# Choosing the place of a first ramp so that four ramps fit one instruction, with a new table for the planner

## The chip, the cores and the metric

One core of a Trainium2 chip. The metric is the time of one execution on the device, in microseconds. The core's engines are called here as the profile calls them: PE (TensorE, matrix products; PEld is its loading of weights), ACT (ScalarE), DVE (VectorE), POOL (GpSimd) and SP (SyncE, which issues the DMAs).

## What is computed

Two layers, each of a multi-query attention (32 heads of 16 columns that share one key and one value head) and a gated MLP with a spatial product over the sequence. The input x is 2048 x 512 in bf16.

```python
def _A_ref(x, wq, wk, wv, wo):
    q = (x @ wq).reshape(B, S, H, Dh)          # H = 32, Dh = 16
    k, v = x @ wk, x @ wv                      # one head
    p = softmax(einsum('bhqd,bkd->bhqk', q, k) * Dh ** -0.5)
    return einsum('bhqk,bkd->bhqd', p, v).reshape(B, S, H * Dh) @ wo

def _B_ref(x, w_in, w_sp, b_sp, w_out):
    z = gelu(x @ w_in)                         # 2 x 896 columns
    g = einsum('ts,bsf->btf', w_sp, layernorm(z[..., 896:])) + b_sp
    return (z[..., :896] * g) @ w_out

for _ in range(2):
    x = x + _A_ref(layernorm(x), ...)
    x = x + _B_ref(layernorm(x), ...)
```

## The kernel before

**Blocks.** The scores of a layer are cut into 2048 blocks of 128 keys by 512 columns (query rows times heads), so 4096 in all. A score matmul (line 2501) makes one block in one of the eight banks of PSUM; up to four stand in a pack and use different rows of PE. A block is then exponentiated into one of 41 places of `Pb` in SBUF (128 x 512 bf16 each, `NPS`), and PV matmuls (line 2758) multiply the places with the values into a bank that gathers four head groups. The values carry a column of ones, so that the denominators come with the products.

**Two ways to exponentiate.** On ACT a block is one Exp from PSUM into a place (line 2698), or two blocks of neighbouring banks go in one instruction (line 2699). [...] A block given to DVE becomes three ramps in int16, whose bits read as bf16 approximate an exponential each; their weighted sum, by weights that three variants of the values hold, is close to the exponential. The first ramp (line 2590, `dve_block` and `first_fn`) reads PSUM and frees the bank. The second and the third (tag "S") read the place of the first and write places of their own; POOL or DVE may take them. A first ramp's place becomes free again when both ramps that read it and its own PV matmul are done.

**Ramps in one instruction.** `commit_ramp` looks for waiting ramps of the same number. Two can always go together (`two`, a step from place to place). Four go together when their sources form a regular box, that is, when of the four places in order the first and the last add up to as much as the two in the middle (`box`), and when four free places form a box too (`free_quad`); the access pattern then has two steps (`quad`). In the profile all of these stand at line 2610 (`ramps_fn`), and their form tells how many: 128x1024 is two, 128x2048 four. A ramp alone is at line 2594. Before the change a first ramp takes the place that has been free longest (`free_slots(1)[0]`).

**The order.** No instruction order is written by hand. While the program is built, a planner (`Sched`, `Kernel.run`) steps through time with a cost for each kind of instruction, and whenever an engine is free in its model, picks what it does next; the order on each engine and the semaphore waits are thereby fixed. For each stretch of 1250 ns of the planner's own time (`STEP`) `follow` sets parameters from `PLAN`: the share of blocks that go to DVE (`SHARE`), how many blocks an Exp may take (`ACT_MAX`), how long a score pack waits to be filled (`FILL_MIN`), whether POOL and DVE may take four ramps at once (`QUADP`, `QUADD`), and some twenty more. A DVE ramp is planned only where POOL is idle in the model, and POOL's next instruction waits for it.

**The stages.** In each layer keys and queries are made first (ramp-up: two groups of blocks run over all keys while keys still arrive). Then packs, exponentials and PV run through all blocks; projections, layer norms, MLP products and spatial products (lines 2181, 2259, 2315, 2354, 2383) are fitted in between on PE. When the last chunk of queries is done, its normalisation, projection, layer norm and MLP follow in a chain, with spatial products beside it (between the layers: the bridge; at the end: the tail). In the second layer's ramp-up no block goes to DVE.

Of the kernel before, what the change touches and what calls it, by code (L numbers as in the profile page):

```python
# [74 lines left out]
def c_mm(n, cols):  # L75
# [8 lines left out]
    11: dict(SLACK=450, PV_MAX=3, PV_LEAST=4),  # L84
    12: dict(SLACK=350, SLACK_HI=400, DVE_LEAD=300),
    13: dict(SLACK=350, SLACK_HI=400, ACT_LOW=1700, FILL_BUSY=4, DVE_LEAD=300, DVE_HIGH=1200),
    14: dict(FILL_MIN=3, MISC_T=2500, QUADD=0),
    15: dict(ACT_LOW=900, PV_LEAST=8),
    16: dict(ACT_LOW=900, PV_LEAST=8, HOLD=400),
    17: dict(ACT_LOW=900, PV_LEAST=8, POOL_TOP=2500, HOLD=400),  # L90
    18: dict(ACT_LOW=900, PV_LEAST=8, SHARE=0.24, POOL_TOP=2500, HOLD=400),
    19: dict(SLACK=450, ACT_LOW=900, PV_LEAST=8, SHARE=0.24, POOL_TOP=2500, HOLD=400),
    20: dict(SLACK=350, SLACK_HI=650, PV_LEAST=4, SHARE=0.24, DVE_LEAD=300, POOL_TOP=2500, MISC_T=700, QUADD=0),
    21: dict(SLACK=350, SLACK_HI=650, PV_LEAST=4, SHARE=0.24, POOL_TOP=2500, MISC_T=700, COLS=2900, DVE_HIGH=1200, QUADD=0),
    22: dict(SLACK=350, SLACK_HI=650, PV_LEAST=4, PV_EFF=0.8, SHARE=0.24, POOL_TOP=2500, MISC_T=700, COLS=2900, DVE_HIGH=1200, QUADD=0),
    23: dict(SLACK=350, SLACK_HI=650, PV_LEAST=4, PV_EFF=0.8, SHARE=0.24, POOL_TOP=2500, MISC_T=700, COLS=2900, DVE_HIGH=1200, QUADD=0),
    24: dict(SLACK_HI=300, ACT_LOW=1700, SHARE=0.31, SCORE_CAP=5, COLS=0, QUADP=0),
    25: dict(SLACK_HI=300, ACT_LOW=1700, SHARE=0.31, SCORE_CAP=5, COLS=0, QUADP=0),
    26: dict(SLACK_HI=300, ACT_LOW=1700, PV_EFF=0.8, SHARE=0.31, SCORE_CAP=5, COLS=0, QUADP=0),
    27: dict(SLACK_HI=300, PV_LEAST=4, COLS=0),  # L100
    28: dict(SLACK=450, FILL_MIN=3, MISC_T=2500),
    29: dict(SLACK=450, FILL_MIN=3, MISC_T=2500, ACT_MAX=1),
    30: dict(PV_LEAST=4),
    31: dict(ACT_MAX=1, QUADD=0),
    32: dict(FILL_MIN=3),
    33: dict(PV_LEAST=4),
    34: dict(PV_LEAST=4, POOL_TOP=3500),
    35: dict(SLACK_HI=400, PV_LEAST=4, POOL_TOP=3500),
    36: dict(SLACK_HI=400, ACT_LOW=1700, PV_LEAST=4, POOL_TOP=3500),
    37: dict(SLACK_HI=400, ACT_LOW=1700, FILL_BUSY=4, PV_LEAST=4, POOL_TOP=3500),  # L110
    38: dict(SLACK_HI=300, PV_MAX=4, PV_LEAST=8, POOL_TOP=2500, ACT_MAX=1, SCORE_CAP=7, DVE_HIGH=2400),
    40: dict(PV_EFF=0.8),
    41: dict(PV_LEAST=4, PV_EFF=0.8),
    42: dict(PV_LEAST=4),
    43: dict(PV_LEAST=4),
    44: dict(PV_LEAST=4, PV_EFF=0.8, MISC_T=700, SCORE_CAP=7),
    45: dict(PV_LEAST=4, PV_EFF=0.8, DVE_LEAD=-600, POOL_TOP=7000, MISC_T=700, SCORE_CAP=7),
    47: dict(PV_MAX=1),
    48: dict(PV_MAX=1),
    49: dict(ACT_LOW=900, COLS=3300, QUADD=0),  # L120
    50: dict(SLACK=600, ACT_LOW=900, FILL_MIN=4, PV_MAX=1, SHARE=0.36, HOLD=400, COLS=0, QUADP=0),
    51: dict(SLACK=600, ACT_LOW=900, FILL_MIN=4, PV_MAX=1, PV_LEAST=4, SHARE=0.36, POOL_TOP=2500, HOLD=400, SCORE_CAP=5, COLS=0, QUADP=0),
    52: dict(SLACK=600, ACT_LOW=900, FILL_MIN=4, PV_MAX=1, PV_LEAST=4, SHARE=0.36, POOL_TOP=2500, HOLD=400, MISC_T=700, SCORE_CAP=5, COLS=0, QUADP=0),
    53: dict(PV_MAX=3, QUADD=0),
    54: dict(FILL_MIN=4, HOLD=400),
    56: dict(SLACK_HI=650),
    58: dict(SLACK_HI=400),
    59: dict(SLACK_HI=400),
    60: dict(SLACK_HI=400),
    61: dict(SLACK_HI=400, PV_MAX=1),  # L130
    62: dict(SLACK_HI=400, PV_MAX=1, MISC_T=2500),
    63: dict(SLACK_HI=400, PV_MAX=1, PV_LEAST=8, PV_EFF=0.8, MISC_T=2500),
    65: dict(PV_LEAST=8),
    66: dict(PV_LEAST=8, POOL_TOP=7000),
    68: dict(FILL_MIN=3, PV_LEAST=4),
    69: dict(PV_EFF=0.8, POOL_TOP=7000),
    70: dict(PV_EFF=0.8, POOL_TOP=7000),
    71: dict(PV_LEAST=8),
    72: dict(PV_LEAST=4, POOL_TOP=2500),
    73: dict(PV_LEAST=4, SHARE=0.24, POOL_TOP=2500),  # L140
    74: dict(FILL_BUSY=3, DVE_LEAD=300),
    75: dict(FILL_BUSY=3, PV_MAX=1, PV_LEAST=8, DVE_LEAD=300),
    76: dict(FILL_MIN=4, FILL_BUSY=3, PV_MAX=1, PV_LEAST=8, DVE_LEAD=300, MISC_T=700),
    77: dict(FILL_MIN=3, FILL_BUSY=3, PV_MAX=1, PV_LEAST=8, SHARE=0.4, DVE_LEAD=300, MISC_T=700),
    78: dict(POOL_TOP=2500),
    80: dict(ACT_LOW=1700, SHARE=0.31, DVE_LEAD=-600),
    81: dict(FILL_MIN=3),
    83: dict(SLACK=450, PV_EFF=0.8, DVE_LEAD=-300),
    85: dict(SLACK=200, SLACK_HI=300, FILL_MIN=3, POOL_TOP=3500),
    86: dict(SLACK=200, SLACK_HI=300, FILL_MIN=3, PV_MAX=3, POOL_TOP=7000),  # L150
    87: dict(SLACK=200, SLACK_HI=300, FILL_MIN=3, PV_MAX=3, POOL_TOP=7000),
    88: dict(PV_MAX=1, DVE_LEAD=-300, DVE_HIGH=2400),
    89: dict(SLACK_HI=800, SHARE=0.24),
    91: dict(HOLD=0, QUADP=0),
    92: dict(DVE_LEAD=-600),
    93: dict(SLACK=450, SHARE=0.24),
    94: dict(ACT_LOW=1700, FILL_MIN=4, PV_MAX=3),
    95: dict(ACT_LOW=500, PV_EFF=0.8, MISC_T=2500),
    96: dict(ACT_LOW=1700, QUADP=0),
    97: dict(HOLD=0, QUADD=0),  # L160
    99: dict(FILL_BUSY=4, DVE_LEAD=300),
    100: dict(FILL_BUSY=4, DVE_LEAD=300, HOLD=0),
    101: dict(FILL_BUSY=4, PV_MAX=1, DVE_LEAD=300, HOLD=0, SCORE_CAP=7),
    103: dict(QUADP=0, QUADD=0),
    104: dict(ACT_LOW=900, PV_MAX=1, QUADD=0),
    105: dict(FILL_BUSY=3, SHARE=0.4, HOLD=400, QUADP=0),
    106: dict(FILL_BUSY=3, PV_LEAST=4, SHARE=0.4, HOLD=400, QUADP=0),
    107: dict(PV_LEAST=4, SHARE=0.4, HOLD=400, QUADP=0),
    108: dict(PV_LEAST=4, SHARE=0.4, HOLD=400, QUADP=0, QUADD=0),
    109: dict(ACT_LOW=1700, PV_LEAST=4, SHARE=0.4, DVE_LEAD=300, HOLD=400, QUADD=0),  # L170
    110: dict(SHARE=0.28),
    112: dict(SLACK=450, SLACK_HI=800, ACT_LOW=1050, PV_LEAST=8, POOL_TOP=2500, HOLD=400, MISC_T=2500, SCORE_CAP=5, DVE_HIGH=1200, QUADD=0),
# [163 lines left out]
    289: dict(FILL_MIN=3),  # L336
    291: dict(DVE_LEAD=-300),
    293: dict(ACT_LOW=1400, FILL_MIN=3, MISC_T=700, DVE_HIGH=2400),
    294: dict(PV_MAX=1, SCORE_CAP=7),
    295: dict(PV_MAX=4),  # L340
    297: dict(QUADD=0),
    298: dict(QUADD=0),
# [2863 lines left out]
```

## Time and profile before

| | |
|---|---|
| runs | 1473.71, 1475.56, 1475.73 us; median 1475.56 us |
| profiled execution | 1473.03 us, its span 1471.3 us |
| instructions | 35574 |
| clock granted to PE | 0.999 of full speed |

The span is the time from the first to the last instruction that the profile has; the execution's own time is 1.7 us longer. A row of instruction groups has the line, the engine, the operation, output and input with their shapes, the count, then busy us and the mean duration in ns, then the engine's idle time before these instructions and what ended it. A row of a stretch has its bounds, its length and the busy time of PE, PEld, DVE, ACT and POOL with the number of instructions, then clock, DMA share and GB/s. A row of waits has who waited, for whom, the total in us, how often, and the longest. Instructions of one engine overlap somewhat in these records, so that a mean duration can be longer than the distance from one start to the next.

### The profile page before, as it was taken

The numbers are of one execution on the slowest core, as the hardware profiler recorded it, in microseconds if no ns is written. First come the engines' busy times: TensorE is split into PE (matmuls) and PEld (weight loads), VectorE is DVE, ScalarE is ACT, GpSimd is POOL, SyncE is SP. The second block draws the span as 40 slices with busy tenths as digits, with TensorE's granted clock in tenths as the row PEclk, the third lists the DMA queues.
The fourth block names the chain that finished last, engine by engine and source line by source line (L and its number), as shares of the span: only waits on it lengthen the run. The fifth ranks groups of instructions, "written<-read, shape, count | busy, mean of one in ns | idle before, by whom it ended". The sixth has DMA issues, their size and how long they took to land.

```text
span 1471.3 us, 35574 instructions
## 1 busy us (share of the span) xinstructions
PE 1428.3 (97%) x14110; PEld 466.5 (32%) x14110; DVE 1397.3 (95%) x2655; ACT 1376.3 (94%) x1712; POOL 1028.8 (70%) x1143
## 2 busy tenths in 40 slices
PE   8999999999999999999999999999999999999999
PEld 3333222222222322234543322222222223223245
DVE  8999999999999999999767999999999999999986
ACT  7999999999999999996589999999999999999950
POOL 6777767777677688774115777777886786787837
PEclk9999999999999999999999999999999999999999
DMA  5330001101011111111121011011010111211111
GB/s 117 66 102 12 16 12 23 34 16 34 19 30 31 23 33 37 31 26 35 22 44 31 16 16 16 12 20 37 16 30 19 33 31 23 34 34 27 33 34 58
DMA packets 155618, 47.02 MB, mean 32 GB/s; under 512 B 148800, under 2 KB 154816, under 8 KB 155456
## 3 DMA queue, kind: packets, MB, share of 16 engines
q1 hardware_dynamic: 155456, 44.75, 15.3%
q8 instruction: 115, 1.88, 0.5%
q14 instruction: 47, 0.39, 0.1%
HBM read 6.46 MB, written 2.10 MB: 6 GB/s over the span
## 4 chain that ended last, share of the span: by engine, by line
ACT 81%; PE 15%; DVE 2%; POOL 1%; DMA 1%; issue 1%
ACT Pb L2699 67%; ACT Pb L2698 9%; PE ps_all L2501 3%; PE ps_all L2383 3%; PE ps_all L2758 3%; PE ps_all L2315 2%; ACT z L2273 2%; PE ps_all L2354 2%; ACT L3001 1%; ACT z L2204 1%; POOL Pb L2610 1%; DVE gp L2325 1%; PE ps_all L2181 1%; DMA z<-xn 1%; ACT z L2186 1%
## 5 line engine op out<-in xcount | busy, mean ns | idle before, releaser
L2699 ACT ACTIVATE Pb<-ps_all 128x1024 bf16<-128x1024 f32 x1214 | 1157.1, 1156 | 3.8 <-PE ps_all L2501 3.3
L2610 POOL TENSOR_SCALAR Pb<-Pb 128x1024 int16<-128x1024 int16 (+1 forms) x738 | 809.3, 1097 | 210.9 <-DVE Pb L2610 161.9
L2590 DVE TENSOR_SCALAR Pb<-ps_all 128x512 int16<-128x512 f32 x1322 | 856.9, 685 | 17.9 <-PE ps_all L2501 10.8
L2501 PE MATMUL ps_all<-z,kT 32*128 32x512 bf16 x4096 | 535.3, 385 | 28.9 <-ACT Pb L2699 15.1
L2758 PE MATMUL ps_all<-Pb,V 128*32 128x512 bf16 x6740 | 521.9, 384 | 2.9 <-ACT Pb L2698 1.5
L2501 PEld LDWEIGHTS ps_all<-z,kT 32*128 32x128 bf16 x4096 | 136.0, 90 | 558.3 <-ACT Pb L2699 379.8
L2315 PE MATMUL ps_all<-wstr,z 128*128 128x512 bf16 x784 | 223.1, 383 | 0.6
L2698 ACT ACTIVATE Pb<-ps_all 128x512 bf16<-128x512 f32 x346 | 213.1, 716 | 5.5 <-PE ps_all L2501 5.5
L2758 PEld LDWEIGHTS ps_all<-Pb,V 128*32 128x32 bf16 x6740 | 124.3, 94 | 220.0 <-issue 123.2
L2610 DVE TENSOR_SCALAR Pb<-Pb 128x1024 int16<-128x1024 int16 (+1 forms) x457 | 192.7, 456 | 0.1
L2325 DVE TENSOR_TENSOR gp<-ps_all,gp 128x512 f16<-128x512 f32 x168 | 113.0, 682 | 1.3 <-PE ps_all L2315 1.0
L2315 PEld LDWEIGHTS ps_all<-wstr,z 128*128 128x128 bf16 x784 | 52.0, 97 | 91.4 <-issue 40.0
L1738 POOL TENSOR_SCALAR ln_rs<-ln_mv 128x1 f32<-128x1 f32 (+1 forms) x60 | 13.2, 223 | 96.4 <-DVE ln_mv L1748 89.5
L2181 PE MATMUL ps_all<-w_in,xnT 128*128 128x448 bf16 x256 | 65.9, 356 | 0.8 <-ACT xnT L1799 0.7
L2383 PE MATMUL ps_all<-w_out,z 128*128 128x512 bf16 x224 | 58.2, 380 | 0.3 <-DVE z L2362 0.3
L2259 PE MATMUL ps_all<-xnT,w_in 128*128 128x512 bf16 (+3 forms) x336 | 52.4, 308 | 0.3 <-ACT z L2186 0.3
L2594 POOL TENSOR_SCALAR Pb<-Pb 128x512 int16<-128x512 int16 x48 | 29.6, 617 | 32.8 <-DVE Pb L2610 14.8
L1978 DVE CAST oT<-ps_all 128x512 bf16<-128x512 f32 x64 | 43.8, 685 | 4.5 <-PE ps_all L2758 4.5
L2141 POOL TENSOR_TENSOR o_norm<-oP,rdn 128x256 bf16<-128x256 bf16 (+1 forms) x76 | 38.3, 528 | 12.8 <-DVE Pb L2610 11.1
L1747 DVE BATCH_NORM_STATS2 ln_st<-X 128x6 f32<-128x512 bf16 x64 | 43.4, 684 | 1.8 <-DMA X<-in_A_x_dram 1.4
L1739 POOL TENSOR_TENSOR ln_rs<-ln_rs,mhalf 128x1 f32<-128x1 f32 (+1 forms) x60 | 34.7, 581 | 11.6 <-DVE Pb L2610 8.5
L2211 DVE BATCH_NORM_STATS2 st<-z 128x6 f32<-128x448 bf16 x64 | 35.4, 607 | 4.5 <-ACT z L2204 4.2
(78 smaller groups left out, 790.0 us busy)
## 6 DMA issues: line engine op xcount, KB each, us to landing
out_dram<-X SPq DMA_DIRECT2D x16, 128.0 KB, 1.7
w_in<-in_B_w_in_dram SPq DMA_DIRECT2D x1, 1792.0 KB, 10.3
X<-in_A_x_dram SPq DMA_DIRECT2D x3, 512.0 KB, 6.5
oP<-oT SPq DMA_TRANSPOSE x60, 2.4
w_out<-in_B_w_out_dram SPq DMA_DIRECT2D x1, 896.0 KB, 12.3
wstr<-in_B_w_sp_dram SPq DMA_TRANSPOSE x40, 4.1
X<-in_A_x_dram SPq DMA_DIRECT2D x2, 256.0 KB, 3.2
wq<-in_A_wq_dram SPq DMA_DIRECT2D x1, 512.0 KB, 4.6
```

The lines of the kernel that those rows point to most:

```text
L1978: ev = Task("dve", c_ps(512), lambda e, u=u, k=k: e.tensor_copy(self.oT[:, k, :], self.ps32[:, u.bank.i, :]), [self.oT_use[k]], 0.2, tag=" ...
L2181: ins = e.matmul(self.ps32[:, b, 0:448], self.xnT2[:, buf, kd, o:o + P], self.w_in[:, kd, FH + h * 448:FH + (h + 1) * 448], start=(kd == 0 ...
L2259: ins = e.matmul(self.ps32[:, b, i * nq:(i + 1) * nq], self.w_in[:, kd, f * P:(f + 1) * P], self.xnT2[:, buf, kd, x0:x0 + nq], start=(kd = ...
L2315: ins = e.matmul(self.ps32[:, b, :], self.z2[:, (s0 + i) % Z2R, f * P:(f + 1) * P], self.wstr[:, sl[i // SLAB][1] + i % SLAB, :], start=(i ...
L2325: return Task("dve", c_ps(512), lambda e: e.tensor_tensor(self.gp[:, tc, f, :], self.ps32[:, bank(), :], src, ALU.add), dps, self.GP_P, ta ...
L2383: ins = e.matmul(self.ps32[:, b, :], self.z1[:, tc, f, o:o + P], self.w_out[:, f, :], start=(f == 0), stop=(f == NF - 1))
L2501: ins = e.matmul(self.ps32[:, jb[i].i, :], self.kT[32 * j:32 * j + 32, u.half, kt * P:(kt + 1) * P], q, tile_position=(32 * j, 0), start=T ...
L2590: return lambda e: e.tensor_scalar(self.Pi[:, dst(), :], self.ps32[:, bank, :], EBIAS + lo, lo, op0=ALU.add, op1=ALU.max)
L2610: return lambda e: e.tensor_scalar(self.several(self.Pi, dst), self.several(self.Pi, src), lo, 1.0, op0=ALU.add, op1=ALU.mult)
L2698: return e.activation(self.Pb[:, ss[0], :], self.ps32[:, bs[0], :], ACTF.Exp, scale=ESCALE)
L2699: return e.activation(self.two(self.Pb, *ss), self.two(self.ps32, *bs), ACTF.Exp, scale=ESCALE)
L2758: ins = e.matmul(self.ps32[32 * j:32 * j + 32, u.bank.i, :], self.V[:, var, kt, :], self.Pb[:, sl.i, :], tile_position=(0, 32 * j), start= ...
```

## The change

A first ramp no longer takes the place that has been free longest. `a_slot` looks at the first 16 free places in the order in which they came free, and at the source places of the ramps that wait (the last six of POOL's list). A place gets 100 points for each three of these sources with which it forms a box, and one point if it forms a box with two of them and another free place; the first of the best is taken. `ASLOT` can switch this off by stretch; no stretch of the table does.

Beside it `PLAN` is another one: 1058 stretches with settings before, 1043 after, nearly all with other values. It decides the order as much as the new function does. The core of the diff:

```diff
@@ PLAN
-    8: dict(ACT_LOW=1400),
-    9: dict(ACT_LOW=1050),
-    10: dict(SLACK=150, FILL_MIN=3, DVE_LEAD=-300, QUADP=0),
...
+    1: dict(FILL_MIN=4),
...
+    14: dict(ACT_LOW=1050, PV_LEAST=4, SHARE=0.4, MISC_T=700, ACT_MAX=1, SCORE_CAP=5, COLS=2900, QUADP=0),
+    15: dict(ACT_LOW=1050, PV_MAX=4, PV_LEAST=4, SHARE=0.4, MISC_T=700, ACT_MAX=1, SCORE_CAP=5, COLS=0, QUADP=0),
...
@@ class Kernel
     QUADD = 1
+    ASLOT = 1
@@ dve_block
         def h0(task, b=None):
-            slot(0, b or self.free_slots(1)[0], task, T)
+            slot(0, self.a_slot(), task, T)
@@
+    def a_slot(self):
+
+        av = self.pslots.avail()[:16]
+        if not self.ASLOT:
+            return av[0]
+        arm = sorted((it[1], it[2].ramp[1][0].i) for it in self.s.arm["pool"] if it[2].ramp is not None and it[2].start is None)
+        pend = []
+        for _, i in arm:
+            if i not in pend:
+                pend.append(i)
+        pend = pend[-6:]
+        best = None
+        for b in av:
+            k = 100 * sum(1 for c in itertools.combinations(pend, 3) if self.box(sorted(c + (b.i,))))
+            if any(x is not b and self.box(sorted(c + (b.i, x.i))) for c in itertools.combinations(pend, 2) for x in av):
+                k += 1
+            if best is None or k > best[0]:
+                best = (k, b)
+        return best[1]
```

More of the change, by code (lines that the diff above doesn't have):

```diff
@@ new lines @@
+    393: dict(PV_MAX=3),
+    394: dict(POOL_TOP=2500, SCORE_CAP=5, DVE_HIGH=1200),
+    395: dict(DVE_LEAD=300, SCORE_CAP=5, COLS=2900),
+    396: dict(FILL_BUSY=4, SCORE_CAP=5),
+    397: dict(MISC_T=700),
+    398: dict(HOLD=400, MISC_T=700, DVE_HIGH=2400),
+    399: dict(COLS=3300),
+    400: dict(PV_LEAST=4, ACT_MAX=1, COLS=3300),
+    401: dict(PV_MAX=1, MISC_T=700),
+    402: dict(FILL_BUSY=3, PV_MAX=3),
+    403: dict(FILL_BUSY=3, PV_MAX=1),
+    404: dict(FILL_MIN=4),
+    405: dict(SLACK_HI=650, FILL_BUSY=4, PV_MAX=1, QUADD=0),
```

2080 lines of the change are left out of this document (1026 added, 1054 removed).

## The prediction

> **What bounds the kernel now.** I read the stage table first, cut where the work changes: start, first attention layer, bridge, second layer's ramp-up, second attention layer, tail. Its columns are the busy us of PE, PEld, DVE, ACT, POOL.
>
> ```profile
> span 1471.3 us, 35574 instructions
> PE 1428.3 (97%) x14110; PEld 466.5 (32%) x14110; DVE 1397.3 (95%) x2655; ACT 1376.3 (94%) x1712; POOL 1028.8 (70%) x1143
> ...
> 20.00:60.00 40.00, 38.04 (x451) 14.19 (x447) 38.86 (x94) 39.93 (x51) 26.90 (x40) 1.00 0.29 51
> 60.00:688.00 628.00, 615.18 (x6024) 180.79 (x6022) 616.31 (x1152) 622.70 (x762) 468.51 (x497) 1.00 0.16 31
> 688.00:717.00 29.00, 28.01 (x263) 18.25 (x262) 24.86 (x52) 6.81 (x12) 4.88 (x12) 1.00 0.13 29
> 717.00:740.00 23.00, 20.80 (x254) 11.94 (x251) 16.82 (x40) 21.71 (x30) 3.47 (x10) 1.00 0.26 36
> 740.00:783.00 43.00, 38.31 (x452) 18.57 (x449) 25.57 (x61) 37.53 (x61) 6.00 (x15) 1.00 0.30 51
> 783.00:1411.00 628.00, 614.66 (x6045) 180.91 (x6038) 613.15 (x1132) 627.60 (x774) 476.36 (x497) 1.00 0.13 24
> 1411.00:1471.30 60.30, 56.07 (x469) 33.83 (x467) 45.87 (x83) 7.94 (x13) 30.66 (x33) 1.00 0.20 55
> ```
>
> Over the whole span PE looks busiest, but the stages differ. In the second layer ACT works 627.60 of 628 us; in the first its missing 5.3 us lie at the end, where the wait for the last chunk begins. In the bridge and the tail ACT hardly works and PE does. The waits of ACT say the same:
>
> ```profile
> ACT xnT L1799 <- PE ps_all L1787: 22.1, 2, 11.2
> ACT z L1799 <- PE ps_all L1787: 17.6, 4, 9.4
> ACT Pb L2698 <- PE ps_all L2501: 5.5, 10, 1.2
> ACT Pb L2699 <- PE ps_all L2501: 3.3, 4, 1.4
> ```
>
> All are waits for PE (total us, times, longest), at the start, the bridge, the ramp-up and the tail. No exponential waits for DVE or POOL. The chain that ended last agrees:
>
> ```profile
> ACT 81%; PE 15%; DVE 2%; POOL 1%; DMA 1%; issue 1%
> ```
>
> So the attention layers last as long as ACT's exponentials, and a ramp made cheaper on POOL or DVE is worth something only where it takes exponentials from ACT.
>
> **The change part by part.** Its arithmetic is the same; what differs is the place that a first ramp takes, the table, and so the whole order. I counted instructions in the orders of both builds, before and after: ramps of two on POOL 692 and 545, of four 46 and 141, of one 48 and 50; on DVE of two 409 and 224, of four 48 and 119, of one 18 and 20; first ramps 1322 and 1324; exponentials of two blocks 1214 and 1229, of one 346 and 314; PV matmuls 6740 and 6744. Everything else has equal counts, DMA issues included. That the change does what it says is thus settled: 94 fours become 260. Durations:
>
> ```profile
> L2610 POOL TENSOR_SCALAR Pb<-Pb 128x1024 int16<-128x1024 int16 x692 | 722.0, 1043 | 204.5 <-DVE Pb L2610 159.5 <-PE ps_all L2501 2.5 <-DVE xn L1758 1.8
> L2610 POOL TENSOR_SCALAR Pb<-Pb 128x2048 int16<-128x2048 int16 x46 | 87.3, 1897 | 6.3 <-DVE Pb L2610 2.4 <-PE ps_all L2501 0.6
> L2594 POOL TENSOR_SCALAR Pb<-Pb 128x512 int16<-128x512 int16 x48 | 29.6, 617 | 32.8 <-DVE Pb L2610 14.8 <-DVE Pb L2590 10.8 <-DVE Pb L2594 4.0
> ```
> ```profile
> 300.69 0.42 DVE L2610 TENSOR_SCALAR Pb<-Pb 128x1024 int16<-128x1024 int16 x1
> 301.02 0.69 DVE L2590 TENSOR_SCALAR Pb<-ps_all 128x512 int16<-128x512 f32 x1
> ...
> 316.09 0.68 DVE L2610 TENSOR_SCALAR Pb<-Pb 128x2048 int16<-128x2048 int16 x1
> 316.69 0.68 DVE L2590 TENSOR_SCALAR Pb<-ps_all 128x512 int16<-128x512 f32 x1
> 317.29 0.68 DVE L2325 TENSOR_TENSOR gp<-ps_all,bspc 128x512 f16<-128x512 f32 x1
> ```
>
> On DVE instructions overlap at their ends, so I take start to start: a two 301.02 - 300.69 = 0.33 us, a four 0.60, a first ramp 317.29 - 316.69 = 0.60. DVE: -185 x 0.33 + 71 x 0.60 + 2 x 0.60 = -17.3 us, with half a us for two singles -16.8. POOL, by its means: -147 x 1.043 + 95 x 1.897 + 2 x 0.617 = +28.1 us. So the fours do not shorten POOL's line: the plan hands it more ramps (1704 block ramps against 1616; DVE 944 against 1028).
>
> *DVE's 16.8 us: I take nothing.* It lies beside a saturated ACT (627.60 of 628). It would count if the plan gave DVE more blocks, but only 2 of 4096 move. From the other side: each block moved takes one exponential (about 0.46 us) from ACT.
>
> *POOL's 28 us: I take nothing.* POOL is busy 476.36 of 628 us there; over both layers' 1256 us it has 311 us left, though part of that is waiting for DVE. If that cover were gone, ramps would come late, PV after them, and the places of Pb would stay taken; that is the slower rival.
>
> *ACT.* Its prices:
>
> ```profile
> 388.73 41.25 ACT Pb L2699 x45
> ...
> 429.98 0.49 ACT Pb L2698
> ```
>
> A two costs 41.25/45 = 0.917 us, a one 0.49. In the first layer both builds give ACT 1372 blocks, as 144 ones and 614 twos before and 152 and 610 after: +8 x 0.49 - 4 x 0.917 = +0.25 us. Within it the first 64 blocks worsen (6 ones and 29 twos become 36 and 14: +14.7 - 13.8 = +0.9) and the rest improves. In the second layer 1402 blocks become 1400: 202 ones and 600 twos become 162 and 619: -19.6 + 17.4 = -2.2 us. Of that -12 ones and +6 twos (-0.4) fall in the first 128 blocks, the ramp-up, where ACT waits for PE anyway and the gain may vanish.
>
> *Bridge.* After the first layer's last score matmul PE has 51 spatial matmuls of 512 columns in the order before and 45 after; six move into the first layer, where PE has room beside ACT (615.18 of 628; the six are 1.3 us). One costs
>
> ```profile
> 689.48 4.70 PE L2315 MATMUL ps_all<-wstr,z 128*128 128x512 bf16 x21
> 694.01 0.39 PE L1787 MATMUL ps_all<-ident,xn 128*128 128x128 bf16 x4
> ```
>
> (694.01 - 689.48)/21 = 0.216 us. Three of them stood behind the transposes of xn, where PE waits for ACT in any case; the other three stood ahead of these transposes, where they fill the time of the last chunk's chain (evacuation, normalisation, projection, layer norm on DVE and POOL). Bounds: 0, if this chain sets the pace, and -1.3, if PE does. I take the middle, three of six: -0.6.
>
> *Start.* The table now sets the stretches from 1.25 us on and ACT takes 36 ones among its first 64 blocks. It may starve there, as it does in the ramp-up, where ones are as dense: ACT stands idle 43 - 37.53 = 5.5 us in that row of 43. For the some 30 us of the first 64 blocks (0.46 each) this share bounds the loss at 4; the table may also force ones while ACT is full, which costs the 0.9 already counted. The row 20 to 60 shows no idle time and is the same stage, so I take 0. Below nothing it cannot go: ACT is full from 20 us on.
>
> *Tail.* The PE orders behind the last score are alike but for two PV matmuls more, less than one matmul group, at most a fifth of a us. I take 0.
>
> Sum: +0.25 - 2.2 - 0.6 = -2.55 us. The profiled execution took 1473.03 us (span 1471.3), so 1470.5. The runs shown have a median of 1475.56, 2.5 us above it; against that median the sum gives 1473.0 us, 0.17% less.
>
> **A rule against it.** The trace shows that POOL does not work beside a DVE ramp:
>
> ```profile
> POOL Pb L2610 <- DVE Pb L2610: 161.9, 204, 2.2
> ...
> 301.19 4.41 POOL L2610 TENSOR_SCALAR Pb<-Pb 128x1024 int16<-128x1024 int16 x4 [0.49 <-DVE Pb L2610]
> ```
>
> The DVE ramp of 300.69 ends at 301.11, POOL starts at 301.19. [...] By the rule alone the sum would grow by what DVE loses. In this kernel's numbers: a DVE ramp that came while POOL works waits at most 1.90 us instead of 1.04, and the first ramps behind it in DVE's order wait with it. The 363 DVE ramps after would have to lose half of that difference, 0.43 us, in 39 cases before the 16.8 us saved are used up. Up to that point the sum stays as it is, since DVE's saving was taken at nothing.
>
> **Rivals.** *DVE's room pays (faster).* For it: DVE is 95% busy, and PE's score matmuls sometimes wait for it. Against: ACT's waits name only PE. If 16.8 us on DVE come back as ACT's share of the work does (the part in which ACT isn't full: the start, 20 us, and the ramp-up, 66 us), at most the 8.8 us that exponentials wait for score matmuls could go. But no L2610 ramp stands between 688 and 783 us at all:
>
> ```profile
> 688.00:717.00 29.00, 0.00 (x0) 0.00 (x0) 1.00 0.13 29
> 717.00:740.00 23.00, 0.00 (x0) 0.00 (x0) 1.00 0.26 36
> 740.00:783.00 43.00, 0.00 (x0) 0.00 (x0) 1.00 0.30 51
> ```
>
> so it is the new order, not the fours, that could take half of the 8.8: 1473.0 - 4.4 = 1468.6.
>
> *Fours tie up places and ACT runs dry (slower).* A four needs a box of four free places at once and holds four sources and four results for 1.90 us, where the earlier of two twos is done after 1.04: its results and their PV come 0.85 us later. There are 41 places; ACT cannot start without one, and behind it wait the banks, and PE's scores. For it: 166 more fours, and the 161.9 us that POOL already waits for DVE's ramps. Against: ACT never waited for a place before, with 94 fours. Price 0.85 us for each POOL four of the 95 more at which no place is free. From 3 such cases the gain is gone, from 6 or 7 the kernel is slower by over 0.2%; one in ten gives 9.5 x 0.85 = 8 us: 1481.
>
> *Nothing is left (same).* The -2.2 comes from how exponentials pair, which is settled where ACT has little choice; a starving start (up to 4 us) eats it: 1475.
>
> **How the numbers follow.** Forecast 0.55, DVE's room or the order 0.17, dry places 0.16, nothing left 0.12. A difference under 0.2% (3 us) is about what a measurement of this kernel cannot tell from none. The forecast's -2.55 lies close to that bound, with a spread of 2 us from the bridge, the start and the runs: 0.22 of its 0.55 is faster, 0.33 the same. With 0.16 of the order rival, faster is 0.38; same 0.33 + 0.11 + 0.02 = 0.46; slower 0.16. The range takes in the forecast, the order rival and nothing left, with the spread of the runs (1473.71 to 1475.73) around them, and leaves out most of dry places: 1467.5 to 1478.
>
> **What would show it.** ACT busy without idle time in both layers, 1229 twos and 314 ones; POOL's ramp time up by about 28 us, DVE's down by about 17, and the span hardly moved. The start's idle time of ACT within 1 us of before; bridge shorter by at most 1.3. Wrong, if exponentials wait for DVE, POOL or PV in the middle of a layer (places), if ACT idles between 10 and 40 us (start), or if the second layer's ramp-up changes its length by more than 2 us.

## The result and the profile after

| | runs | median us | lowest to highest |
|---|---|---|---|
| before | 11 | 1474.32 | 1472.83 to 1475.73 |
| after | 11 | 1483.87 | 1473.67 to 1487.41 |

The ratio is 1.006, with an interval of 1.0049 to 1.0071: the changed kernel is slower by 9.5 us, outside the range predicted. Its runs are of two kinds: one took 1473.67 us at a mean granted PE clock of 0.999, the other ten 1482.27 to 1487.41 us at 0.984 to 0.988. The profile is of the one short run, so it can't show what the other ten do. Its page and chain:

```profile
span 1471.9 us, 35327 instructions
PE 1405.9 (96%) x13971; PEld 463.7 (32%) x14114; DVE 1386.7 (94%) x2545; ACT 1375.1 (93%) x1695; POOL 1056.8 (72%) x1093
...
ACT 56%; PE 32%; DVE 9%; issue 1%; DMA 1%; POOL 1%; POOLq 0%; DVEq 0%
```

Its stage table, cut as that of before (length, then busy us of PE, PEld, DVE, ACT, POOL; then the clock):

```profile
20.00:60.00 40.00, 38.17 (x444) 13.40 (x443) 37.82 (x91) 40.00 (x60) 28.26 (x41) 1.00 0.23 48
60.00:688.00 628.00, 603.97 (x5981) 179.45 (x6039) 612.18 (x1099) 624.83 (x757) 482.36 (x478) 1.00 0.15 31
688.00:717.00 29.00, 27.38 (x245) 17.99 (x248) 25.07 (x51) 6.04 (x11) 3.54 (x9) 1.00 0.19 40
717.00:740.00 23.00, 20.95 (x244) 12.31 (x245) 17.13 (x42) 19.43 (x30) 4.50 (x12) 1.00 0.20 30
740.00:783.00 43.00, 38.72 (x457) 19.53 (x463) 25.76 (x63) 38.34 (x55) 6.31 (x16) 1.00 0.26 53
783.00:1411.00 628.00, 604.42 (x5990) 179.38 (x6052) 608.10 (x1081) 627.64 (x762) 489.58 (x467) 1.00 0.13 24
```

And ACT's waits:

```profile
ACT xnT L1785 <- PE ps_all L1773: 21.4, 2, 10.7
ACT z L1785 <- PE ps_all L1773: 17.8, 4, 9.2
ACT Pb L2705 <- PE ps_all L2487: 6.6, 11, 1.4
ACT Pb L2704 <- PE ps_all L2487: 4.0, 7, 0.9
```

In this execution ACT is full in both layers as forecast, it waits for PE alone, and no exponential waits for a place. The span is 0.6 us above that of before, where 2.55 less was forecast. (PE's 603.97 us against 615.18 before is no saving: of 14114 matmuls 143 records are missing, as PE's count beside PEld's shows. The chain that ended last goes through PE for 32% of the span, before for 15%; why was not followed up.) So the 9.5 us are not in what this profile shows. What the clocks of the other ten runs suggest, and the experiments test, is a stretch at half clock. Both traces at hand show two levels of the clock only, 1.00 and 0.50; by these a run of 1482 us at 0.986 has spent some (1 - 0.986) x 1482 / 0.5 = 41 us at half clock. The trace of before has one stretch at half clock within its span, 3.413 us from 954.4 us on; that of this short run one too, from 385.9 us on.

### The profile page after: what moved, and what is told of

It is laid out like the page before. It is cut to its first block, busy times and chain, and to the rows that moved or that the text cites. A ratio compares the mean times of both kernels' runs of the same rounds, so it can differ in the third digit from the quotient of the medians.

```text
span 1471.9 us, 35327 instructions
## 1 busy us (share of the span) xinstructions
PE 1405.9 (96%) x13971; PEld 463.7 (32%) x14114; DVE 1386.7 (94%) x2545; ACT 1375.1 (93%) x1695; POOL 1056.8 (72%) x1093
## 4 chain that ended last, share of the span: by engine, by line
ACT 56%; PE 32%; DVE 9%; issue 1%; DMA 1%; POOL 1%; POOLq 0%; DVEq 0%
ACT Pb L2705 46%; PE ps_all L2764 9%; PE ps_all L2487 9%; ACT Pb L2704 6%; PE ps_all L2301 6%; DVE Pb L2576 5%; PE ps_all L2369 3%; PE ps_all L2167 2%; PE ps_all L2340 1%; DVE Pb L2596 1%; ACT z L2259 1%; ACT L3007 1%; DVE gp L2311 1%; DMA z<-xn 1%; PE ps_all L2070 1%
## 5 line engine op out<-in xcount | busy, mean ns | idle before, releaser
L2596 POOL TENSOR_SCALAR Pb<-Pb 128x1024 int16<-128x1024 int16 (+1 forms) x686 | 836.2, 1219 | 172.7 <-DVE Pb L2596 125.8
L2576 DVE TENSOR_SCALAR Pb<-ps_all 128x512 int16<-128x512 f32 x1324 | 858.7, 684 | 25.6 <-PE ps_all L2487 17.8
L2301 PE MATMUL ps_all<-wstr,z 128*128 128x512 bf16 x683 | 201.3, 383 | 17.0 <-issue 11.0
L2704 ACT ACTIVATE Pb<-ps_all 128x512 bf16<-128x512 f32 x314 | 188.7, 718 | 4.2 <-PE ps_all L2487 4.0
L2596 DVE TENSOR_SCALAR Pb<-Pb 128x1024 int16<-128x1024 int16 (+1 forms) x343 | 171.3, 530 | 0.5
L2369 PE MATMUL ps_all<-w_out,z 128*128 128x512 bf16 x206 | 54.9, 380 | 2.8 <-POOL z L2359 0.7
L2245 PE MATMUL ps_all<-xnT,w_in 128*128 128x256 bf16 (+3 forms) x332 | 51.1, 308 | 0.2
L1725 POOL TENSOR_TENSOR ln_rs<-ln_rs,mhalf 128x1 f32<-128x1 f32 (+1 forms) x60 | 34.5, 577 | 10.3 <-DVE Pb L2596 8.0
```

The costliest lines, as they stand in the source:

```text
L2245: ins = e.matmul(self.ps32[:, b, i * nq:(i + 1) * nq], self.w_in[:, kd, f * P:(f + 1) * P], self.xnT2[:, buf, kd, x0:x0 + nq], start=(kd = ...
L2301: ins = e.matmul(self.ps32[:, b, :], self.z2[:, (s0 + i) % Z2R, f * P:(f + 1) * P], self.wstr[:, sl[i // SLAB][1] + i % SLAB, :], start=(i ...
L2369: ins = e.matmul(self.ps32[:, b, :], self.z1[:, tc, f, o:o + P], self.w_out[:, f, :], start=(f == 0), stop=(f == NF - 1))
L2576: return lambda e: e.tensor_scalar(self.Pi[:, dst(), :], self.ps32[:, bank, :], EBIAS + lo, lo, op0=ALU.add, op1=ALU.max)
L2596: return lambda e: e.tensor_scalar(self.several(self.Pi, dst), self.several(self.Pi, src), lo, 1.0, op0=ALU.add, op1=ALU.mult)
L2704: return e.activation(self.Pb[:, ss[0], :], self.ps32[:, bs[0], :], ACTF.Exp, scale=ESCALE)
```

## The experiments

Three theories. **A**: PE has too little to do somewhere at the start and its clock is halved for a while. **B**, the prediction's slower rival: places run dry behind the fours. **C**: single falls of the clock behind the gelu batches (in which ACT computes the MLP's gelu) add up. In the diffs below, which are shortened to what differs, `add_warm` puts extra instructions on PE between two of the order, and nothing else moves: each adds the product of a weight of zeros to a sum that is open, so it changes no value. A group is four such matmuls side by side, like the kernel's own zero-weight groups (line 2889 before, 2895 after).

### The changed kernel again

No edit.

> The changed kernel once more, unaltered, to see a profile of the execution that most of its runs show. Its eleven runs are one of 1473.67 us with a mean granted clock of 0.999, and ten between 1482.3 and 1487.4 with 0.984 to 0.988; the trace so far is of the first. Theory A (the clock): the ten lose their time to some 41 us at half clock, (1 - 0.986) x 1482 / 0.5, twelve stretches of the 3.4 us that the one dip in the trace lasts. It expects clocks of 0.984 to 0.988 again, 1480 to 1488 us, and dips that lie where PE has little to do, first of all behind the gelu batches, as the one dip in the trace does (385.9 us). Theory B (places run dry, the slower rival of the prediction): the longer runs show exponentials that wait for free places or POOL inside a layer, with the low clock as their consequence; it expects ACT idle by 8 to 10 us in the two layers before PE is slowed.

1483.48 us median of 12 runs (before 1473.78, 17 runs), ratio 1.0057 [1.0038, 1.0077]. Two runs had a clock of 1.0 and took 1470.86 and 1471.46; one 1475.84 at 0.996; nine 1481.90 to 1489.44 at 0.980 to 0.988. Seven runs of before at clock 1.0 have a median of 1472.49. So time goes with the clock, and at full clock the new order is about 1.3 us faster, by two runs against seven. The profile caught a short run once more, so this run decides nothing between A and B: in it ACT has no wait inside the layers, but B speaks of the long ones. A long one is shown below.

### The slot alone, and the table alone

```diff
-PLAN = {... after's}          # e2_slot_only
+PLAN = {... before's}
-    ASLOT = 1                 # e3_table_only
+    ASLOT = 0
```

> The new choice of a first ramp's place with the old table. By the order it has 88 fours (before 94, after 260), and 1115 single exponentials instead of 346: the table no longer fits the order. If exponentials set the layers' length, ACT has +769 x 0.49 - 382 x 0.917 = +26.5 us of work: about 1500 us or more, whatever the clock does. If the clock alone decides, it should stay within 10 us of before.

> The new table with the old choice of place (the switch at 0). By the order it has 20 fours and 1025 single exponentials: +679 x 0.49 - 340 x 0.917 = +21 us on ACT, so about 1495 us or more if exponentials set the length; within 10 us of before if not.

1562.89 us (1.0606) and 1567.94 us (1.064), two runs each. ACT's added work of 26.5 and 21 us explains less than a third of that; where the rest lies was not looked into. This separates nothing: each table is fitted to one run of the planner, and with the other slot choice there are only 88 and 20 fours and 1115 and 1025 exponentials of one block (314 with both parts). The change can't be taken apart in this way. But the profile of the second shows what none before it had: half clock from 18.5 us on, for 34.1 us.

### Extra groups at the start, and the same number later

```diff
+        K.add_warm(lambda t: 12000 <= t.start < 18500 and t.tag in ("score", "KV")
+                   or 18500 <= t.start < 40000 and t.tag == "score" and K.few(t))      # e4: ten groups
+        K.add_warm(late)      # e5: ten groups, ahead of score packs from 60 us on
```

> The changed kernel with its order and all its waits kept, and ten groups of four matmuls of zero weights more on PE, which add nothing to a bank that is being summed up: nine between 12.7 and 17.8 us of the plan, one at 30 us. Theory A (a start in which PE does too little lets its granted clock fall to half, and at half clock it stays there for ten windows or so): all runs at a clock of 0.995 or more and a median of 1470.5 to 1473.5 us, 10 us below the changed kernel. Theory B (places of Pb run dry in the layers): no change, 1482 to 1485. Theory C (the low clock comes from the stretches behind the gelu batches): no change either, since nothing is added there.

> The control to the run before: the same ten groups, put at 61.5 to 69.6 us of the plan instead of the start. Theory A: they don't help, most runs at 0.984 to 0.988 and 1482 to 1487 us; 2 us more at most, the time of ten groups at 0.22 us. A theory by which any more work on PE holds the clock: 1471 to 1474.

The ten groups at the start gave 1483.29 us, ratio 1.0047 [1.0029, 1.0066]: four of 12 runs at 1473.39 to 1476.49 (clock 0.999 to 1.0), eight at 1482.16 to 1486.27 (0.987 to 0.992). Not a cure, and its own profile is of a short run. But e7_split (below) has the same ten groups at the start, and its profile is of a long one:

```profile
24.76 0.40 PE L1878 MATMUL ps_all<-z,wk 128*128 128x128 bf16 x4 [1.35 <-DMA z<-xn]
25.27:52.57 27.30, 27.30 (x201) 8.41 (x199) 19.35 (x48) 19.34 (x31) 12.85 (x20) 0.50 0.17 34
```

There the clock holds through the stretch that the groups fill, and falls behind a later wait, at 25.27 us, for 27.30 us: in this run the filler moved the fall and did not remove it. The control gave 1487.1, 1.0086 [1.007, 1.0101], all four runs at 0.985 to 0.987, and its profile is of a long run. Its PE timeline and stretches:

```profile
14.54 0.40 PE L1878 MATMUL ps_all<-z,wk 128*128 128x128 bf16 x4
14.78 0.25 PE L1881 MATMUL ps_all<-wv,z 128*128 128x16 bf16 x4
16.27 0.40 PE L1878 MATMUL ps_all<-z,wk 128*128 128x128 bf16 x4 [1.25 <-DMA z<-xn]
16.51 0.25 PE L1881 MATMUL ps_all<-wv,z 128*128 128x16 bf16 x4
```
```profile
14.42:17.83 3.41, 2.16 (x32) 1.17 (x28) 2.10 (x9) 2.24 (x3) 1.50 (x4) 1.00 0.31 41
17.83:51.97 34.14, 34.14 (x255) 11.30 (x251) 24.68 (x64) 26.44 (x44) 16.14 (x30) 0.50 0.22 36
20.00:60.00 40.00, 39.80 (x333) 12.66 (x329) 30.09 (x73) 32.22 (x50) 19.87 (x31) 0.60 0.24 48
```

Two keys tasks (the products that make keys and values, lines 1878 and 1881) stand next to each other on PE, and the second waits 1.25 us for its transposing DMA, so that PE works 2.16 of the 3.41 us. The clock is then at half for ten times 3.413 us, though PE is busy in all of it, and ACT gets 32.22 us of work into the 40 us in which the short run had 40.00. What ACT waits for between 17.8 and 52 us is PE's scores, 8.5 us in all:

```profile
ACT Pb L2706 <- PE ps_all L2489: 5.0, 9, 1.2
ACT Pb L2707 <- PE ps_all L2489: 3.5, 4, 1.2
```

In the layers behind it, too, this long run has exponentials wait for scores alone (1.6 us in the first layer, 2.0 in the second), and none for a place, POOL or DVE. That speaks against B.

The time at which the n-th exponential ends (counted from 0) shows where that is lost; each column is the difference to the short profile of after, in us:

| exponential | short run ends it at | e5_late_warm | e10_burst | e8_cure | e12_keys_pairs | e13_split_pool | e14_split_dve |
|---|---|---|---|---|---|---|---|
| 10 | 20.4 | 0.1 | 0.4 | 0.5 | 0.1 | 0.4 | 0.6 |
| 30 | 31.9 | 4.8 | 5.4 | 2.9 | 2.5 | 2.8 | 3.0 |
| 50 | 43.4 | 10.3 | 5.7 | 5.5 | 2.6 | 5.4 | 5.6 |
| 400 | 360.1 | 13.4 | 5.7 | 5.6 | 2.6 | 7.3 | 5.8 |
| 500 | 455.3 | 12.1 | 4.3 | 4.2 | 1.3 | 6.7 | 5.8 |
| 1540 | 1410.0 | 14.7 | 3.9 | 4.5 | 0.5 | 22.1 | 6.8 |

In e5_late_warm 10.3 us are gone by the fiftieth; the rest comes with the ten added groups and three later windows at half clock. (Between 400 and 500 four columns fall by some 1.3 us: that is the short run's own half clock at 385.9 us, the price of one window. The last column has a fall of its own there.) So a single window in mid-layer is worth about 1.3 us, all that C can offer, and the start about 10.

### Before with less for PE to do

```diff
+            if t is not None and t.tag == "warm" and not t.first and 12500 <= t.start < 24000:     # e6: nine groups
+            if t is not None and t.tag == "warm" and not t.first and t.start < 48000:              # e9: 18 groups
+                K.s.prog["pe"][i] = (p[0], K.extra_fn(t.ug, (0,)), p[2], t)      # one matmul of four
```

> The kernel before, with order and waits kept, and nine of its groups of four zero matmuls between 12.5 and 24 us of the plan cut to one matmul each. Nothing of the change is in it. Theory A: part or most of the runs fall to clocks of 0.983 to 0.990 and 1480 to 1487 us, and the profile, if it catches one, has PE at half clock from about 16 to 50 us. Theory B and C: 1472 to 1476 as before.

> The kernel before, order and waits kept, with all its zero-weight groups up to 48 us but the first of each bank cut from four matmuls to one (18 groups; the run before this one cut nine). Theory A: PE now does as little as in the changed kernel, and at least a third of the runs fall: granted clock 0.98 to 0.99, 1481 to 1487, median 1473 to 1484. Rival (the fall belongs to the new order by itself, whatever PE does): no run under 0.995, median 1472 to 1475, ratio 0.999 to 1.001.

1473.14 us, 0.9993 [0.9984, 1.0002], and 1474.32 us, 0.9996 [0.9984, 1.0008]; every clock 0.995 or more. Theory A missed twice. The second one's profile says why:

```profile
13.66:17.08 3.42, 2.36 (x26) 1.26 (x26) 3.00 (x10) 3.35 (x6) 2.37 (x5) 1.00 0.22 44
17.08:20.49 3.41, 3.41 (x29) 1.28 (x28) 2.25 (x9) 2.79 (x3) 2.00 (x6) 0.50 0.14 28
20.49:23.90 3.41, 3.36 (x34) 1.18 (x32) 3.41 (x11) 3.10 (x4) 0.71 (x3) 1.00 0.29 58
```

The clock does fall, at the same place, but it is back after one window. What PE did in that window at half clock (groups of PE; the first shape is rows by columns of the weights):

```profile
L2760 PE MATMUL ps_all<-Pb,V 128*32 128x512 bf16 x12 | 1.9, 627 | 0.0
L2503 PE MATMUL ps_all<-z,kT 32*128 32x512 bf16 x7 | 1.1, 544 | 0.0
L3121 PE MATMUL ps_all<-wq,zero 128*32 128x512 bf16 x2 | 1.1, 535 | 0.0
L1892 PE MATMUL ps_all<-z,wk 128*128 128x128 bf16 x4 | 0.6, 308 | 0.0
L1895 PE MATMUL ps_all<-wv,z 128*128 128x16 bf16 x4 | 0.3, 186 | 0.0
```

Mostly matmuls on all 128 rows (called full-row work here); only the score matmuls use 32. This gave theory **A2**: the fall is found in both orders (in that of before once its groups are thinned), and what differs is how soon the clock comes back, which hangs on full-row work, not on PE being busy. To size it I took from 16 traces (those of the runs below among them), window by window of 3.413 us, the share of time in which full-row work streams. (The stretches at half clock last one, two, eight, nine or ten times that: 3.413 us in before, 6.83 in e10_burst, 27.30 in e7_split, 30.72 in e11_before_thin, 34.14 in e5_late_warm.) A matmul is given a time by its columns: in the trace of before, matmuls in a row start 0.216 us apart at full clock for 512 columns, 0.109 for 256 and 0.055 for 128, and 0.43 apart for 512 at half clock (at 954.46 and 954.89 us). One on 32 rows counts a quarter, and four of these side by side add up to one; column strips side by side count once. At full clock 18 windows were followed by half clock, with shares of 0.14 to 0.384; of some 6850 that were not, the lowest have 0.366, 0.367, 0.367, 0.376 and 0.381. At half clock 37 windows were followed by another one, with shares up to 0.715; 18 were followed by full clock, 14 of them at 0.748 to 0.977. Four rose at 0.61 to 0.70, all after 200 us; these the measure does not explain. So in these traces about 0.38 keeps the clock and about 0.75 gets it back, which would be the same full-row work per window. That the rows matter shows when every matmul counts alike: then 122 windows that kept the clock lie below the highest that lost it, by rows only the five named, and 11 instead of four of those that rose lie below the highest that stayed. The quarter itself is a choice of mine that nothing here measures.

### A cure against the fall

```diff
+        K.add_warm(lambda t: 0 if not 12000 <= t.start < 47000 else 2 if t.tag == "KV" else int(
+            t.tag == "score" and (t.start < 18500 or K.few(t))))      # 39 groups
```

> The changed kernel with its order and its waits, and 39 extra groups of four matmuls on zeros (each adds nothing to a sum that is open) between 12 and 47 us: two ahead of each keys task, one ahead of a score pack where the stretch before it is thin. Theory A (PE does too little in some stretch of 3.4 us between 15 and 25 us, and the granted clock then stays at half until about 50 us): no run falls, every granted clock is 0.996 or more, median 1470.5 to 1474.5, ratio 0.997 to 1.000. Rival (the fall comes from something else in the new order, such as the fours or the late transfer by itself): 8 to 9 runs in 12 still at 0.98 to 0.99 and 1481 to 1488, ratio 1.005. If extra matmuls themselves delay ACT's scores at the start by 39 x 0.2 us with nothing gained, 1475 to 1479 at a clock of 1.0.

1480.48 us, 1.0034 [1.0021, 1.0047]; clocks 0.995 to 1.0 in all nine runs. The long kind of run is gone, as A has it, but the median isn't 1470.5 to 1474.5: the case set apart at the end of the expectation, that the extras delay ACT, came with it, and costs more than its 1479.

```profile
13.00:17.00 4.00, 3.95 (x60) 1.71 (x56) 2.89 (x11) 2.69 (x5) 2.02 (x4) 1.00 0.65 47
...
20.00:60.00 40.00, 39.55 (x497) 13.49 (x494) 33.72 (x83) 35.76 (x54) 24.30 (x35) 1.00 0.25 48
```

With the 39 groups PE is full at full clock, 39.55 of 40.00 us where the short run had 38.17, and ACT loses 40.00 - 35.76 = 4.2 us there. PE has no room for them in this start even at full clock.

### A burst behind the fall, and before made thin

```diff
+        at = [19000, 24000]               # e10: seven groups ahead of the score pack at each
+        def burst(t):
+            if at and t.tag == "score" and t.start >= at[0]:
+                at.pop(0)
+                return 7
+            return 0
+        K.add_warm(burst)
```
```diff
         # e11: e9_before_cold, and six matmuls of zeros on 32 rows
+        K.add_warm(lambda t: int(t.tag == "score" and 15500 <= t.start < 21000))
```

> The changed kernel, order and waits kept, and nothing against the fall itself: only two bursts of seven extra zero-weight groups, one ahead of the score pack planned at 19 us and one ahead of that at 24 us. Theory A2 (one thin window of 3.413 us at 13 to 19 us sets the clock to half, as it does in the kernel before too; what differs is the stretch behind it, in which PE at half clock has to stream full-row work in three quarters of a window before the clock comes back, and the changed kernel's packs give only 0.60 to 0.70): the first burst ends the stretch after one to three windows, every granted clock is 0.994 or more, and the median is 1472 to 1477 (14 groups of 0.22 us cost up to 3 us where ACT is kept waiting), ratio 0.999 to 1.002. Rival (the fall has to be avoided, and once there it lasts whatever PE does): two thirds of the runs at 0.98 to 0.99 and 1482 to 1488, ratio 1.005 to 1.009.

> The kernel before with its zero-weight groups up to 48 us thinned as in the run before, and six added matmuls of zeros on 32 rows alone, ahead of the score packs between 15.5 and 21 us: PE has more to do, but what it does there uses a quarter of its rows. Theory A2: the window behind the fall, in which the thinned kernel before had 0.80 of full-row work at half clock and so rose again after one window, goes to about 0.6, and the half clock lasts 6 to 12 windows in a third to two thirds of the runs: those at 0.980 to 0.99 and 1480 to 1488. Rival (the long stretch belongs to the changed order): no run under 0.994, median 1473 to 1476, ratio 0.999 to 1.001 (the six matmuls of 0.21 us cost at most 1.3 us).

The burst: 1479.26 us, 1.0035 [1.0022, 1.0047], clocks 0.992 to 0.998, where the changed kernel had 0.980 to 0.988 in nine of 12, so the long stretch is cut short with the fall left in. Three of the eight clocks lie below the 0.994 forecast, and the median missed its 1477: by the fiftieth exponential two windows and 14 groups have cost 5.7 us. Its profile has half clock in two windows, 18.22 to 25.05 us, and the second is filled by the burst (groups of PE there, seven added groups and two of the kernel's own):

```profile
L3127 PE MATMUL ps_all<-wq,zero 128*32 128x512 bf16 x28 | 3.2, 634 | 0.0
L2898 PE MATMUL ps_all<-wq,zero 128*32 128x512 bf16 x8 | 1.0, 621 | 0.0
```

Before made thin: 1480.51 us, 1.0038 [1.0022, 1.0055]; runs from 1473.14 (clock 1.0) to 1487.12, three of the 12 at 0.988 to 0.990 with 1484.59 to 1487.12, five at 0.993 to 0.995. Three of 12 is less than the third that was forecast, but the rival's "no run under 0.994" is out. Six matmuls of 0.21 us, 1.3 us of work, lengthen single runs by up to 13 us (against 1474.32 without them). In its profile:

```profile
17.05:47.77 30.72, 30.72 (x186) 9.11 (x189) 18.48 (x52) 19.95 (x20) 12.76 (x26) 0.50 0.21 40
```
```profile
L2503 PE MATMUL ps_all<-z,kT 32*128 32x512 bf16 x6 | 1.8, 602 | 0.0
L3121 PE MATMUL ps_all<-wq,zero 32*32 32x512 bf16 x3 | 1.6, 531 | 0.0
L3121 PE MATMUL ps_all<-wq,zero 128*32 128x512 bf16 x2 | 1.2, 608 | 0.0
L2760 PE MATMUL ps_all<-Pb,V 128*32 128x512 bf16 x3 | 0.6, 607 | 0.0
```

The first row is the stretch, nine windows; the others are the groups of its first window, in which nine of 14 matmuls use 32 rows (share 0.40, where the kernel without them had 0.80). The order of before, given more but thinner work for PE, shows the long stretch; the changed order, given full-row work, loses it. Both directions bear A2 out, though its sizes were missed in both.

### A cheaper cure

```diff
+        K.add_warm(lambda t: 2 if t.tag == "KV" and 12000 <= t.start < 28000 else 0)      # 16 groups
```

> The changed kernel, order and waits kept, with 16 extra zero-weight groups: two ahead of each of the eight keys tasks planned between 12 and 28 us, where PE can wait for a transfer, and none ahead of score packs. Theory A2 says that with the thin windows filled there is no fall, and that what the kernel then costs is what the extras cost ACT: granted clocks of 0.995 or more, and 1472 to 1477, less than the 39 groups of the stronger version (1480.5), ratio 0.998 to 1.002. Rival (a fall needs more than these 16 groups against it): a mixture, a third or more of the runs at 0.985 to 0.992 and 1481 to 1486.

1475.39 us (before 1473.61), 1.0011 [1.0001, 1.0021]; 11 of 12 runs at 0.996 to 1.0 and 1473.80 to 1476.38, one at 0.992 and 1481.07. Groups where PE would wait for the transfer anyway bring back 7.8 of the 9.5 us (9.5 - 1.8); its profile is 2.6 us behind the short run by the fiftieth exponential. It does not beat before: at full clock the new order is worth about 1.3 us by the two runs above, and the groups cost more.

### Fours issued as two twos

```diff
+        if len(g) == 4:                      # e7, on e4_start_warm
+        if len(g) == 4 and eng == "pool":    # e13, on e8_cure; "dve" in e14
+            two = [self.ramps_fn(v, ...first two...), self.ramps_fn(v, ...last two...)]
```

> The changed kernel with the ten groups at the start, order kept, and each of its 260 ramps of four issued as two ramps of two in a row. POOL gets 141 x (2 x 1.043 - 1.897) = 27 us more, DVE 119 x (2 x 0.33 - 0.60) = 7 us. If ACT alone sets the length of the layers and POOL has room: within 2 us of the run without the split. If the fours carry the gain: 5 us or more slower. If fours tie up places (the slower rival of the prediction): faster.

> The changed kernel with the 39 extra groups (clock at full) and each four of POOL issued as two twos; DVE's fours stay. POOL gets 141 more instructions, 141 x (2 x 1043 - 1899) = 26 us more busy time. If POOL's spare 28% covers this, as the prediction took for granted: 1479 to 1483, ratio 1.002 to 1.006, as with the fours. If the order uses POOL's room up (rival): 1488 to 1500.

> The same with DVE's fours split and POOL's kept: 119 more instructions, 119 x (2 x 423 - 693) = 18 us more of DVE. If DVE's time is worth nothing, as the prediction took it: 1479 to 1483. If DVE, 94% busy, is part of what sets the layers' length: 1486 to 1498. The splits of both engines together cost 20 us on a kernel whose clock had fallen; the two parts should add to about that.

Both engines' fours split: 1504.89 us, 1.0201 [1.0181, 1.0221], some 21 us above the runs of the kernel under it at the same clock (1483.1 to 1484.1 at 0.989 to 0.991): the case "the fours carry the gain". POOL's alone: 1496.48, 1.016 [1.0146, 1.0175], 16.0 us over its base of 1480.48. DVE's alone: 1481.76, 1.0058 [1.0045, 1.0071], 1.3 us over. (The base was run beside other runs of before; set against its own runs of before, each split is 17.1 and 2.4 us over.) The parts add to 17 to 20, the two together to 21. The page of the second, with the chain:

```profile
PE 1436.6 (96%) x14270; PEld 465.4 (31%) x14270; DVE 1404.7 (94%) x2545; ACT 1384.2 (93%) x1695; POOL 1091.9 (73%) x1234
...
PE 49%; DVE 21%; ACT 18%; POOL 9%; issue 2%; DMA 1%; POOLq 0%
```

The waits of PV for POOL's ramps, in the base (line 2767) and with the split (line 2773):

```profile
PEld ps_all L2767 <- POOL Pb L2599: 21.9, 93, 0.6
...
PE ps_all L2767 <- POOL Pb L2599: 0.3, 1, 0.3
```
```profile
PEld ps_all L2773 <- POOL Pb L2599: 51.7, 155, 1.5
...
PE ps_all L2773 <- POOL Pb L2599: 10.7, 31, 1.2
```

POOL is busy in 73% of the span and still late: PV waits for its ramps, PE works in its fixed order, score packs come behind the PV, and ACT's share of the chain goes from 54% to 18%. The loss is spread over both layers, 6.9 us in the first and 10.6 in the second from first to last exponential.

This run isn't POOL's time alone, however. DVE's own fours, which were not touched, also take longer (base, then split):

```profile
L2599 DVE TENSOR_SCALAR Pb<-Pb 128x2048 int16<-128x2048 int16 x119 | 84.3, 724 | 0.2
```
```profile
L2599 DVE TENSOR_SCALAR Pb<-Pb 128x2048 int16<-128x2048 int16 x119 | 92.8, 793 | 3.3 <-POOL Pb L2599 3.1
```

DVE ramps that start while POOL is at work last longer, mostly by what POOL has left less 0.14 us; in this trace that adds up to 25.8 us, in the base to 6.4. DVE's busy time rises by 17.3 us and POOL's by 35.1, not 26. How the 16 us divide between late POOL ramps and longer DVE ramps is not separated.

## Why the prediction was wrong

**The step that failed** is the start: "The row 20 to 60 shows no idle time and is the same stage, so I take 0." The 0 is right for ACT's supply at full clock (40.00 of 40 in the profiled run). It took PE's speed for given. In 19 of 23 runs of the changed kernel the clock was below 0.99. No profile caught a long run of the kernel as it is; the long run with the same start (e5_late_warm, altered only behind 60 us) had PE at half clock for 34.14 us and lost 10.3 us by the fiftieth exponential, and with the start filled (e12_keys_pairs) the clock stayed up in 11 of 12 runs and 7.8 of the 9.5 us came back. The bound that I gave, 4 us, came from ones that starve ACT; no bound was set for PE.

What could have been seen: between 12 and 24 us the orders differ in full-row work. These are the zero-weight matmuls in that stretch, of before and of after:

```profile
L2889 PE MATMUL ps_all<-wq,zero 128*32 128x512 bf16 x40 | 4.0, 388 | 0.0
```
```profile
L2895 PE MATMUL ps_all<-wq,zero 128*32 128x512 bf16 x28 | 2.6, 387 | 0.0
```

The orders of both builds, which were at hand, show the same, and in the changed one the two keys tasks side by side, whose second needs a transfer. The wait itself is not new (before's profile has it with 0.66 us, at 15.42 us); there is less full-row work around it. Between 10 and 50 us the lowest share of a window is 0.43 in before's profile and 0.387 in after's; the window ahead of the fall in the long run has 0.325. The prediction looked for what stands behind ACT's waits, not PE's. The count alone would not have done, though: thinned before has 11 such matmuls in this stretch and does not lengthen, since its clock rises again. Why the transfer lands late in some runs (a wait of at most 0.3 us in the short profile of the repeat, 1.07 in that of after, 1.25 in the long one) stays open. So does why after's own profile kept its clock with that wait: its window from 13.8 us has the share of 0.387, hardly above the falls, and where the windows begin differs between runs: the first change to half clock comes at 17.05 us in e11_before_thin, 17.08 in e9_before_cold, 17.83 in e5_late_warm and 18.22 in e10_burst. Ahead of the falls in the start of e9_before_cold, e10_burst and e11_before_thin a keys task waits as well, 0.98, 1.23 and 1.14 us.

**The other steps.** *What bounds it:* right at full clock. *Counts and durations:* POOL rose from 1028.8 to 1056.8 us, +28.0 (predicted +28.1); DVE fell by 10.6 (predicted 16.8 from start to start; the rest is not accounted for). *ACT, bridge and tail:* -2.55 us in sum; runs at clock 1.0 give about -1.3. By stages, the repeat's profile, which has no half clock in its span, can be set beside that of before. From first to last exponential the first layer takes 671.6 us against 670.2, +1.4 (predicted +0.25). The second takes 692.1 against 694.5; without before's one window at half clock (some 1.3 us) that is about -1.1 (predicted -2.2). Between the layers ACT has 35.5 us without an exponential against 36.5, -1.0 (predicted -0.6, bounds 0 and -1.3). Behind the last exponential there are 60.1 us against 59.7, +0.4 (predicted 0). Each term was good to about 1.2 us, and all are too small to matter beside the start.

*DVE's 17 us at nothing:* borne out as far as tested. Splitting DVE's fours gave DVE 6.4 us more busy time (1387.4 to 1393.8; the 18 of the expectation counts overlapping ends twice), which cost 1.3 to 2.4 us. *POOL's 28 us at nothing:* the result was right, the reason wrong. "POOL has 311 us left" is no cover: POOL's fours split in the same order cost 16.0 us, some of it perhaps by way of DVE's longer ramps. That the new order carries its 28 us because the planner, which knew them, put other work beside them is argued, not tested.

*The rule against it* (POOL does not work beside a DVE ramp): the traces show it from both sides, and it is small here. In the profile of before no POOL instruction starts within any of the 475 DVE ramps, and a two of DVE that starts at 502.28 us, with 1.02 us of a POOL four still to come, takes 1.30 us instead of 0.42. In the profile of after, DVE ramps that start while POOL is at work lose 6.5 us in all, before 3.8; the longest one, a four at 210.40 us, takes 1.12 us more than usual, with 1.26 us of POOL's four still to come. That is far from the 16.8 us at which it would have counted.

*The slower rival* named 1481 us by places that run dry. The time came close, the cause didn't: in the short profiles and in the long one (e5_late_warm) no exponential waited for a place, POOL or DVE in a layer. That the number came out was luck. A number that fits does not show a mechanism. And the profile of one execution, which was to decide, was of the rarer kind; the list of runs with their clocks showed the result first.

## What to carry to other kernels

Read the clock of every run ahead of the profile, and when an order changes, ask for each window (3.413 us here) in which PE has much waiting or only part-row matmuls whether it can keep its clock (by these traces a full-row share of about 0.38), and what full-row work behind it would bring the clock back (about 0.75). Here filler paid at the waits: 16 groups placed there brought back 7.8 of 9.5 us, most of which 39 spread ones gave away again (1475.39 us against 1480.48). An engine's idle share is no sure cover for more work on it when others wait for it in a fixed order (POOL, 73% busy: 16.0 us). Splitting its instructions in the same order tests that in one run; look at the other engines' durations there too.

## What was unexpected of the hardware

- Once fallen in the start, the clock stayed at half for 8 to 10 windows while PE was busy in practically all of that time (27.30 of 27.30 us in e7_split, 30.72 of 30.72 in e11_before_thin, 34.14 of 34.14 in e5_late_warm, and in e3_table_only 30.00 of the 30.00 from 20 to 50 us). In these 16 traces full-row work below about 0.38 of a window lost it, and about 0.75 at half clock brought it back, with four rises that this measure leaves unexplained.
- Matmuls on 32 of 128 rows counted little: with six of them added (1.3 us of PE's work) the clock stayed down for nine windows in the profile of e11_before_thin, where it had risen after one in that of e9_before_cold.
- A wait of PE of about 1 us in a thin window (1.25 us for a transfer in e5_late_warm) stood ahead of a loss of 10 us. That the wait tips the window over is argued from its share, not tested by itself.
- A DVE ramp that started while POOL worked lasted longer by about what POOL had left (1.12 us more with 1.26 us to go).
- One window at half clock in the middle of a layer cost about 1.3 us (the one at 385.9 us in the short run of after), and the kernel before has such windows too (one at 954.4 us): part of the spread of its runs, 1472.17 us at clock 1.0 and 1479.81 at 0.994.
